# Attention with an expert stage on one core: five token sets for six, and split up-weights kept in DRAM

## The chip, the core and the metric

The kernel runs on one core of a Trainium2 chip. The metric is the time of one execution in device microseconds (us); lower is better. TensorE does the matmuls, VectorE, ScalarE and POOL (GpSimd) the elementwise work, SP (SyncE) issues most DMAs, and POOL issues some on a queue of its own, where descriptors are made in software.

## The reference, cut to what matters

```python
scores = scale * np.matmul(q, k.transpose(0, 1, 3, 2)) + bias.transpose(2, 0, 1)[None]
attn = softmax(scores)                      # batch 8, heads 8, 576 x 576
x = np.matmul(attn, v)                      # gathered to 4608 tokens x 512
a = x @ w1                                  # 512 -> 1024
b = x @ w2                                  # 512 -> 1024
h = a * b @ w3                              # 1024 -> 1024
return h @ w_out                            # 1024 -> 512
```

The weights of the expert stage come as 64-bit floats and are narrowed on the chip.

## The kernel before, in words

Attention runs first, 32 units of one head pair and one batch. It leaves unscaled rows of x (x_d, one tensor for each of four head pairs) and the reciprocal row sums (r_d) in DRAM. Under its end, and after it, w3 and w_out are folded into one down-weight by matmuls (fold, L775; their bank is wacc), so that the expert stage is two products: up (x with w1 and w2, then the product g of both) and down (g with the folded weight).

Every fp32 operand is split into a rounded high part and a low part (split, L904: ScalarE copies, VectorE subtracts), and a product is three matmuls of 128x128 weights with a moving tile of some columns (times, L1053). The expert stage goes over the 4608 tokens in six sets of 768 (TOK, L727). Each set is two halves of 384 tokens, and 384 is the number of columns of a matmul. Up and down are done as 2x2 block products with seven products for eight (seven, L1068; Winograd's form, named "1" to "7"), which needs sums of blocks of both operands. The first set's up-product alone is done with eight (plain_step, L1113), as its weights are just being narrowed: 8 steps of 48 matmuls. Later sets take 8 up steps of 42 matmuls (up_step, L1136) and every set 168 for down (down_step, L1160).

Of a set's x, four rows groups are loaded into the tile xr, and the matching reciprocal sums, broadcast, into xs (fetch in x_units, L922, with load_x, L808, and load_r, L814: one DMA of x and two of r each, all on SP's queue). POOL scales (L819) and makes the block sums (L935), and seven units are split into xu, a ring of nine units. The same ring holds the 14 units of g.

Up-weights: the first set narrows blocks 3 to 7 while it computes (narrowed, L1001: a fetch from the input, two ScalarE, four VectorE and two POOL steps for each half) and stores all eight, unsplit, in wu_d (L1033). Each later set loads each of the eight again, 0.5 MB (L1039), POOL makes four sums (L1045), ScalarE and VectorE split into ub and ut (up_ring, L1037). Down-weights are split once, stored in dw_d and loaded seven times a set, 1 MB each, by POOL's queue (fetch_down, L1224).

Products leave the PSUM banks b through ScalarE's copy into one of eight buffers wos (take, L1063, the copy is L1066); VectorE adds, and SP stores to out from the same buffer (L1187).

A planner (Planner, L112) sets the order on each engine, SP's queue among them. Each step has an engine, a supposed duration, the steps it follows and the ring buffers it takes. A step of a ring takes a buffer when the older one's users are done. The planner walks through time and gives each engine the step that can start first; a DMA is costed on its own, with 0.08 us of its queue and the bytes at a fixed rate, whatever else is in flight:

```python
    def dma(b):
        return 2.3 + b / 300e3
...
            clock[s.on] = t + (0.08 if s.on == "SP" else s.us)
```

TensorE's order is written by hand in the last loop of the kernel (work, L1259 to L1267). Each queue issues in order: an instruction that has to wait holds all that stand behind it.

Of the kernel before, what the change touches and what calls it, by code (L numbers as in the profile page):

```python
# [38 lines left out]
    "r0": 0.0, "r1": 0.9, "r2": 1.8, "r3": 2.7, "h0": 3.6, "h1": 4.5, "h2": 5.4, "h3": 6.3, "l0": 4.5, "l1": 5.4, "l2": 6.3, "l3": 7.2,  # L39
# [5 lines left out]
PRODUCT = {"1": (0, 1), "2": (1, 2), "6": (2, 4), "5": (3, 3), "7": (4, 5), "3": (5, 0), "4": (6, 6)}  # L45
XU_N, SR_N, FIN_N, BANK_N, WU_N, UB_N, UT_N, DW_N = 9, 6, 8, 8, 4, 3, 2, 4
# [55 lines left out]
class Step:  # L102

    def __init__(self, on, us, run, after, uses, takes, lag):
        self.on, self.us, self.run, self.after, self.takes, self.lag = on, us, run, list(after), list(takes), lag
        self.uses = list(uses) + self.takes
        self.then, self.want, self.start = [], None, None
        for h in self.uses:
            h.users.append(self)


class Planner:  # L112

    LAG = {"PE": 0.25, "SP": 0.0}

# [3 lines left out]
    def step(self, on, us, run, after=(), uses=(), takes=(), lag=None):  # L119
        s = Step(on, us, run, [a for a in after if a is not None], uses, takes, self.LAG.get(on, 0.1) if lag is None else lag)  # L120
        self.steps.append(s)
        return s

    def order(self, pe, bank):
# [39 lines left out]
        clock = {}  # L164
# [14 lines left out]
        while len(out) < len(self.steps):  # L179
            best = None  # L180
            for e, cands in ready.items():
                free = clock.get(e, 0.0)
                picks = []
                for s in cands:
                    if e == "PE" and s is not pe[turn]:
                        continue
                    t = max([free] + [done[b] + (b.lag if b.on != e else 0.0) for b in s.after])
# [52 lines left out]
def relpos_attention_moe(  # L240
# [136 lines left out]
    x_d = [dram.tile([P, NTOK], F32, name=f"x_d{p}") for p in range(NPAIR)]  # L377
    r_d = [dram.tile([2, NTOK], F32, name=f"r_d{p}") for p in range(NPAIR)]
# [348 lines left out]
    TOK = 768  # L727
    CH = TOK // 2
    NPR = NTOK // TOK
# [6 lines left out]
    cv = moe.enter_context(tc.tile_pool(name="cv2", bufs=2, side="right"))  # L736
# [3 lines left out]
    wu_d = [dram.tile([P, 2 * DM], F32, name=f"wu_d{t}") for t in range(NF)]  # L740
    dw_d = [dram.tile([P, 2 * KG * BW], F32, name=f"dw_d{i}") for i in range(7)]
# [14 lines left out]
    fo = ExitStack()  # L756
    fp = fo.enter_context(tc.tile_pool(name="fp", bufs=3, side="right"))
# [11 lines left out]

    def ub(i):  # L770
        if "ub" not in late:
            late["ub"] = gp.tile([P, UB_N, 2, 3, BW], F32R, name="ub")
        return late["ub"][:, i]
# [31 lines left out]
    def xa(t, k):  # L805
        return X["x"][:, k * KH:(k + 1) * KH, t * CH:(t + 1) * CH]

    def load_x(c, cc):  # L808
        nc.sync.dma_start(X["x"][:, cc, :], x_d[cc][:, c * TOK:(c + 1) * TOK])

    def flat(i):
        return X["s"][:, i].rearrange("p k n -> p (k n)")

    def load_r(c, cc, i):  # L814
        for h, rows in enumerate((lo, hi)):
            nc.sync.dma_start(flat(i)[rows], r_d[cc][h:h + 1, c * TOK:(c + 1) * TOK].broadcast_to([64, TOK]))  # L816

    def scale(eng, cc, i):
        eng.tensor_tensor(X["x"][:, cc, :], X["x"][:, cc, :], flat(i), op=ALU.mult)  # L819
# [7 lines left out]
    def unit(i, low):  # L827
        return X["u"][:, i, low]
# [17 lines left out]
    X["s"] = xs.tile([P, SR_N, KH, CH], F32, name="xs")  # L846
    X["u"] = xs.tile([P, XU_N, 2, KH, CH], F32R, name="xu")
    ut = xs.tile([P, UT_N, 2, 4, BW], F32R, name="ut")
# [6 lines left out]
    def first_load():  # L855
        for cc in range(NC):
            load_x(0, cc)
            load_r(0, cc, cc)

# [38 lines left out]
    def dma(b):  # L898
        return 2.3 + b / 300e3
# [444 lines left out]
```

## Time and profile before

| | |
|---|---|
| median of 3 runs | 1139.82 us (1139.54 to 1141.91) |
| profiled execution, its own time | 1143.05 us |
| its span | 1141.3 us |
| mean granted TensorE clock | 0.964 |
| busy: TensorE, VectorE, ScalarE, POOL | 92%, 77%, 62%, 52% |
| DMA | 199.79 MB, mean 175 GB/s |

The span goes from the first to the last instruction of the profiled execution; a little time lies around it, so its own time is longer. A busy share is a mean over stages with different limits. Attention and the fold take the span up to about 517 us, the expert stage the rest. An "idle before" with an arrow names what ended the wait.

### The profile page before, as it was taken

How to read it: one execution, taken by the hardware profiler on the slowest of the kernel's cores; microseconds unless marked ns; L12 is line 12 of the kernel's file. 1: busy time of each engine (PE TensorE's matmuls, PEld its weight loads, DVE VectorE, ACT ScalarE, POOL GpSimd, SP SyncE). 2: the span in 40 equal slices, each digit the busy share in tenths (PEclk: the TensorE clock that was granted, in tenths of full speed). 3: DMA queues.
4: the chain of work that ended last, by engine and by line, in shares of the span. 5: the costliest groups of instructions: out<-in, count | busy, mean ns of one | idle time of the engine just before them, and what ended most of it. 6: DMA issues, size and time to landing. Idle time of an engine off the chain costs nothing.

```text
span 1141.3 us, 24384 instructions
## 1 busy us (share of the span) xinstructions
PE 1051.1 (92%) x9448; PEld 913.2 (80%) x9448; DVE 879.8 (77%) x1592; ACT 706.2 (62%) x1292; POOL 588.7 (52%) x486
## 2 busy tenths in 40 slices
PE   6979999999999999997778989979996996999998
PEld 2367777777777777676668979979996996999998
DVE  8958887888888888483898748957885794787775
ACT  8779988998998998552524534624552472455433
POOL 0076766776776775403584357337436542743310
PEclk9989999999999999998888989999998998899999
DMA  7955574566557452158567763592286259228205
GB/s 231 318 162 172 177 238 144 174 211 210 160 174 233 160 172 94 52 155 249 194 239 286 262 191 92 160 288 88 73 277 186 74 177 275 83 61 272 75 1 166
DMA packets 72866, 199.79 MB, mean 175 GB/s; under 512 B 10800, under 2 KB 25520, under 8 KB 66480
## 3 DMA queue, kind: packets, MB, share of 16 engines
q1 hardware_dynamic: 65248, 150.39, 42.3%
q0 software_dynamic: 6496, 45.94, 12.2%
q10 hardware_dynamic: 1008, 1.92, 0.6%
q8 instruction: 74, 1.21, 0.5%
q14 instruction: 40, 0.33, 0.1%
HBM read 156.77 MB, written 41.45 MB: 174 GB/s over the span
## 4 chain that ended last, share of the span: by engine, by line
PE 71%; DVE 12%; DMA 10%; issue 3%; ACT 2%; SPq 2%; POOL 1%; DVEq 0%; ACTq 0%; POOLq 0%
PE b L1055 33%; PE pst L574 14%; PE s L463 13%; PE pst L515 6%; DMA xs<-r_d 5%; PE wacc L798 4%; DVE zdve L665 3%; DMA out_dram<-wos 2%; DVE xu L910 2%; DMA ub<-in_moe_w_dram 1%; DVE ut L910 1%; DMA nb_d<-bev 1%; DVE ub L318 1%; SPq L816 1%; DVE w3s L910 1%
## 5 line engine op out<-in xcount | busy, mean ns | idle before, releaser
L1055 PE MATMUL b<-xu,ut 128*128 128x384 f32 x1344 | 265.5, 349 | 65.6 <-ACT wos L1066 35.6
L1055 PEld LDWEIGHTS b<-xu,ut 128*128 128x128 f32 x1344 | 248.4, 197 | 70.3 <-ACT wos L1066 36.9
L474 DVE CUSTOM_DVE_ANT_0 ts<-s,nb 128x576 f32<-128x576 f32 x288 | 210.6, 756 | 53.7 <-PE s L463 21.3
L499 ACT ACTIVATE pp<-ts,mx 128x576 f32<-128x576 f32 x256 | 195.9, 769 | 17.1 <-DVE mx L474 17.1
L902 DVE TENSOR_TENSOR wos<-b,wos 128x384 f32<-128x384 f32 x156 | 84.4, 553 | 125.1 <-PE b L1055 117.1
L1055 PE MATMUL b<-xu,w3s 128*128 128x384 f32 x1008 | 179.2, 334 | 0.0
L1055 PEld LDWEIGHTS b<-xu,w3s 128*128 128x128 f32 x1008 | 175.4, 188 | 0.0
L574 PE MATMUL pst<-pt,rv 128*64 128x320 f32 (+1 forms) x1280 | 169.3, 411 | 1.3 <-ACT pt L542 1.3
L1066 ACT COPY wos<-b 128x384 f32<-128x384 f32 x183 | 86.6, 477 | 119.4 <-PE b L1055 74.2
L542 ACT ACTIVATE pt<-pst 128x1024 f32<-128x1024 f32 x128 | 128.5, 1021 | 28.4 <-PE pst L515 26.2
L1055 PE MATMUL b<-xu,ub 128*128 128x384 f32 x720 | 141.4, 341 | 0.0
L574 PEld LDWEIGHTS pst<-pt,rv 128*64 128x64 f32 x1280 | 86.3, 136 | 62.4 <-issue 9.7
L1045 POOL TENSOR_TENSOR wi<-wu 128x256 f32<-128x256 f32 x80 | 83.6, 1064 | 99.7 <-DVE ut L910 96.9
L1055 PEld LDWEIGHTS b<-xu,ub 128*128 128x128 f32 x720 | 129.2, 192 | 0.0
L463 PE MATMUL s<-kh,qh 64*128 64x288 f32 x640 | 116.3, 356 | 6.8 <-DVE mx L474 6.7
L822 ACT ACTIVATE ub<-wu 128x768 fp32r<-128x768 f32 x40 | 34.0, 849 | 113.7 <-PE b L1055 101.4
L515 PE MATMUL pst<-ident,pp 64*128 64x64 f32 x2304 | 102.4, 223 | 1.1 <-ACT pt L542 0.6
L515 PEld LDWEIGHTS pst<-ident,pp 64*128 64x128 f32 x2304 | 100.0, 140 | 3.3 <-ACT pt L542 1.2
L540 DVE COPY pt<-pst 64x64 f32<-64x64 f32 (+3 forms) x160 | 82.1, 514 | 25.3 <-PE pst L574 18.9
L463 PE MATMUL s<-kh,ql 64*128 64x288 f32 x640 | 97.2, 294 | 0.9 <-DVE ql L444 0.9
L463 PE MATMUL s<-kl,qh 64*128 64x288 f32 x640 | 97.1, 294 | 0.0
L819 POOL TENSOR_TENSOR xr<-xr,xs 128x768 f32<-128x768 f32 x20 | 39.2, 1961 | 104.4 <-DMA xs<-r_d 104.4
(118 smaller groups left out, 1855.2 us busy)
## 6 DMA issues: line engine op xcount, KB each, us to landing
w3s<-dw_d POOLq DMA_DIRECT2D x42, 1024.0 KB, 6.1
wu<-wu_d SPq DMA_DIRECT2D x40, 512.0 KB
rq<-in_q_dram SPq DMA_DIRECT2D x28, 640.0 KB
wi<-in_moe_w_dram SPq DMA_DIRECT2D x22, 512.0 KB
nb_d<-bev SPq DMA_DIRECT2D x36, 295.5 KB
rv<-in_v_dram SPq DMA_DIRECT2D x32, 320.0 KB
x_d<-pt SPq DMA_DIRECT2D x32, 288.0 KB
xr<-x_d SPq DMA_DIRECT2D x24, 384.0 KB
```

The lines of the kernel that those rows point to most:

```text
L463: nc.tensor.matmul(s[:, hf, :HS], Q[x][rows, q0:q0 + P], K[y][rows, h * HS:(h + 1) * HS], start=(m == 0), stop=(m == len(ops) - 1),)
L474: nc.vector.tensor_tensor_reduce(out=halves(ts), in0=d.pop(("s", t))[:, :, :HS], in1=halves(NB[p, t]), op0=ALU.add, op1=ALU.min, scale=-1. ...
L499: nc.scalar.activation(pp, ts, AF.Exp, bias=mx, scale=-1.0, accum_out=sums[p][:, 9 * b + col:9 * b + col + 1])
L515: nc.tensor.transpose(ps[0:n, hf, c0:c0 + 64], x[rows], ident[rows, rows])
L540: nc.vector.tensor_copy(o, x)
L542: nc.scalar.activation(o, x, AF.Copy)
L574: nc.tensor.matmul(o, x[:, c0:c0 + D], m, start=(c == 0), stop=(c == 4))
L798: nc.tensor.matmul(wacc[ft], l[:, n * P:(n + 1) * P], r[t], start=(t == 0 and m == 0), stop=(t == NF - 1 and m == 2),)
L902: return lambda: nc.vector.tensor_tensor(o(), a(), b(), op=op)
L1045: nc.gpsimd.tensor_tensor(o, x, y, op=ALU.subtract)
L1055: nc.tensor.matmul(acc, w(l), x(r), start=start and i == 0, stop=stop and i == 2, skip_group_check=True)
L1066: return h, pl.step("ACT", 0.16 + CH / 1200, lambda: nc.scalar.copy(fin[h.at], banks[src.at]), after, [src], [h])
```

## The change

Five token sets of 912, 924, 924, 924 and 924 tokens replace six of 768, so a matmul has 456 or 462 columns. The number of matmuls in the expert stage goes from 3072 to 2568 (384 plain, 4 x 336 up, 5 x 168 down).

Split up-weights: the second set loads the unsplit blocks, splits three of them, makes the sums in place and splits these, all in one buffer w of seven blocks (up_sums), and stores that buffer, 1.835 MB, in ws_d. The three sets behind it load whole buffers (up_whole) on POOL's queue and split nothing. The ring w has three buffers; the rings ub and ut go.

From the third set on x and r are loaded by POOL's queue, each of the four behind a load of a weight buffer of the set in front (pace); the second set's are loaded by SP. Scaling and block sums of x move from POOL to VectorE. The ring xu has eight units; four of them, and xr, are lent to the narrowing in the first set, so g is split there only when all blocks are narrowed (first_s). Two of the split down-weights stay in SBUF from the first split on, and their order of making is turned round.

The planner counts transfers: one wire for all DMAs (first byte 2.0 us, then the bytes one after the other), at most eight unfinished DMAs in a queue, and 0.6 us of the queue for each.

```diff
-PRODUCT = {"1": (0, 1), "2": (1, 2), "6": (2, 4), "5": (3, 3), "7": (4, 5), "3": (5, 0), "4": (6, 6)}
-XU_N, SR_N, FIN_N, BANK_N, WU_N, UB_N, UT_N, DW_N = 9, 6, 8, 8, 4, 3, 2, 4
+PRODUCT = {"1": (0, 1), "2": (1, 2), "6": (2, 4), "5": (3, 5), "7": (4, 3), "3": (5, 0), "4": (6, 6)}
+TOKENS = 912, 924, 924, 924, 924
+XU_N, FIRST_U, FIN_N, BANK_N, WU_N, HELD_W, W_N, DW_N = 8, 4, 8, 8, 3, 3, 3, 4
...
+        self.busy = 0.6 * lanes if mb else us
+        self.us = Planner.FIRST_BYTE + mb / Planner.RATE if mb else us
...
+    FIRST_BYTE, RATE, LANES = 2.0, 300e3, 8
...
+                    if s.mb and len(lanes[e]) >= self.LANES:
+                        t = max(t, lanes[e][-self.LANES])
...
-            clock[s.on] = t + (0.08 if s.on == "SP" else s.us)
+            clock[s.on] = t + s.busy
             done[s] = t + s.us
+            if s.mb:
+                wire = max(wire, t + self.FIRST_BYTE) + s.mb / self.RATE
+                done[s] = s.end = wire
+                lanes[s.on] += [wire] * s.lanes
...
     def x_units(c):
...
-            a = pl.step("SP", dma(8 * P * TOK), fetch, takes=[hx, hs] if cc == 0 else [hs], uses=[] if cc == 0 else [hx])
-            r.append(pl.step("POOL", 0.2 + TOK / 467, lambda cc=cc, hs=hs: scale(nc.gpsimd, cc, hs.at), [a], [hx, hs]))
...
+            on, queue = ("SP", nc.sync) if c == 1 else ("POOL", nc.gpsimd)
+            fetch = pl.step(on, 0.0, lambda cc=cc, queue=queue: load_x(queue, c, cc), () if c == 1 else pace[c - 1][cc:cc + 1], [hx] if cc else (), ([] if cc else [hx]) + [hs[cc]], mb=2 * P * TOKENS[c] * 4, lanes=3)
+            r.append(pl.step("DVE", tt(2 * n), lambda cc=cc: scale(nc.vector, c, cc), [fetch], [hx, hs[cc]]))
...
+    def up_sums(n, hw, kept):
+
+        h7 = R["w"].hold()
+        get = pl.step("SP", 0.0, lambda: nc.sync.dma_start(wu[hw.at], wu_d[n]), kept, takes=[hw], mb=512 << 10)
 
         def sums():
...
+            b = blocks(hw.at)
+            for o, x, y in ((2, 0, 2), (0, 1, 0), (1, 1, 2), (3, 3, 1)):
+                nc.gpsimd.tensor_tensor(b[:, o], b[:, x], b[:, y], op=ALU.subtract)
+
+        w = split(lambda: blocks(hw.at)[:, 1:4], 3 * BW, lambda k: w7(h7.at)[:, k, 0:3], h7, [get], [hw], [h7])
+        s = pl.step("POOL", 4.4, sums, w, [hw])
+        w += split(lambda: blocks(hw.at), 4 * BW, lambda k: w7(h7.at)[:, k, 3:7], h7, [s], [hw])
+        put = store(7 << 18, lambda: nc.sync.dma_start(ws_d[n], f(w7(h7.at))), w, [h7])
+        return h7, w, [put]
+
+
+    def up_whole(n, kept):
+        h7 = R["w"].hold()
+        return h7, [pl.step("POOL", 0.6, lambda: nc.gpsimd.dma_start(w7(h7.at), ws_d[n]), kept, takes=[h7], mb=7 << 18)], []
...
+                if c == 0:
+                    after = list(after) + first_s
...
+            if c == 0:
+                rings = [up_sums(n, R["wu"].hold(), kept[n]) for n in range(NF)]
+                kept = [r[2] for r in rings]
+            else:
+                rings = [up_whole(n, kept[n] if c == 1 else ()) for n in range(NF)]
+            pace[c + 1] = [r[1][0] for r in rings]
```

SP's queue before, at the end of a set's down products (out_dram<-wos is the store of a result, wu<-wu_d an up-weight block, xr and xs the loads of x and r for the set after the next up-products):

```order
L1187 DMA out_dram<-wos_9520 128x384
L1039 DMA wu_8970<-wu_d_8977 128x1024
L809 DMA xr<-x_d_85 128x768
L816 DMA xs<-r_d_89 64x768 x2
L809 DMA xr<-x_d_86 128x768
L816 DMA xs<-r_d_90 64x768 x2
L809 DMA xr<-x_d_87 128x768
L816 DMA xs<-r_d_91 64x768 x2
L809 DMA xr<-x_d_88 128x768
L816 DMA xs<-r_d_92 64x768 x2
L1187 DMA out_dram<-wos_9516 128x384
L1187 DMA out_dram<-wos_9517 128x384
```

SP's queue with the change, from the second set's up steps into its down products (ws_d<-w stores a split buffer):

```order
L1066 DMA ws_d_8973<-w_9517 128x3584
L1056 DMA wu_8961<-wu_d_8968 128x1024
L1066 DMA ws_d_8974<-w_9287 128x3584
L1056 DMA wu_83<-wu_d_8969 128x1024
L1066 DMA ws_d_8975<-w_9517 128x3584
L1066 DMA ws_d_8976<-w_9517 128x3584
L1066 DMA ws_d_8977<-w_9287 128x3584
L1212 DMA out_dram<-wos_9523 128x462
L1212 DMA out_dram<-wos_9524 128x462
```

The loads of x and r are gone from this queue, and behind these rows it holds stores of out alone up to its end.

POOL before, from one set's down products to the next set's up steps:

```order
L1231 DMA w3s_9569<-dw_d_8979 128x2048
L1045 TENSOR_TENSOR wi<-wu_9514 128x256 x2
L1045 TENSOR_TENSOR wi<-wu_9514,wi 128x256 x2
L936 TENSOR_TENSOR xr<-xr,xs 128x2x384
L1231 DMA w3s_10058<-dw_d_8980 128x2048
L1231 DMA w3s_10058<-dw_d_8981 128x2048
L1231 DMA w3s_9569<-dw_d_8982 128x2048
L819 TENSOR_TENSOR xr<-xr,xs 128x768 x4
L936 TENSOR_TENSOR xs<-xr 128x768
L1045 TENSOR_TENSOR wi<-wu_83 128x256 x2
```

POOL with the change, the same place of a later set:

```order
L1263 DMA w3s_10106<-dw_d_8982 128x2048
L1263 DMA w3s_10106<-dw_d_8983 128x2048
L1263 DMA w3s_9561<-dw_d_8984 128x2048
L822 DMA xr<-x_d 128x924
L824 DMA xs<-r_d 64x924 x2
L822 DMA xr<-x_d 128x924
L824 DMA xs<-r_d 64x924 x2
L822 DMA xr<-x_d 128x924
L824 DMA xs<-r_d 64x924 x2
L1072 DMA w_9287<-ws_d_8973 128x3584
L1072 DMA w_9517<-ws_d_8974 128x3584
```

POOL's sums and scalings have left it; three of the four loads of x and r now stand here, ahead of the set's fourth weight buffer.

VectorE with the change, among the up steps of the second set (g<-b and wos<-b read banks, w<-wu is a split of weights):

```order
L841 TENSOR_TENSOR w_9517<-wu_8961,w_9517 128x768
L832 TENSOR_TENSOR xr<-xr,xs 128x924
L918 TENSOR_TENSOR wos_9519<-b_9535,wos_9519 128x462
L918 TENSOR_TENSOR wos_9524<-b_9532,wos_9524 128x462
L918 TENSOR_TENSOR wos_9522<-b_9537,wos_9522 128x462
L841 TENSOR_TENSOR w_9517<-wu_8961,w_9517 128x1024
L918 TENSOR_TENSOR g<-b_9535,wos_9519 128x462
L841 TENSOR_TENSOR w_9287<-wu_83,w_9287 128x768
```

The scaling (L832) that POOL did as L819 stands between the two splits of one weight buffer.

## Rows read from the trace of the kernel before

**Rows 1.** The page's head.

```profile
span 1141.3 us, 24384 instructions
```

**Rows 2.** Timeline of TensorE: start, us, instructions merged, idle before and its end.

```profile
516.92 16.81 PE L1055 MATMUL b<-xu,ut 128*128 128x384 f32 x96
546.08 0.69 PE L1055 MATMUL b<-xu,ut 128*128 128x384 f32 x1 [12.35 <-ACT ut L822]
...
623.59 25.12 PE L1055 MATMUL b<-xu,w3s 128*128 128x384 f32 x144
648.55 1.21 PE L1055 MATMUL b<-xu,ub 128*128 128x384 f32 x6
...
771.84 2.29 PE L1055 MATMUL b<-xu,ut 128*128 128x384 f32 x6 [9.07 <-ACT wos L1066]
...
1136.78 0.68 PE L1055 MATMUL b<-xu,w3s 128*128 128x384 f32 x3
```

**Rows 3.** Windows: length, busy PE PEld DVE ACT POOL, clock, DMA share, GB/s.

```profile
495.00:515.00 20.00, 20.00 (x88) 16.30 (x87) 18.25 (x28) 10.71 (x17) 0.00 (x0) 1.00 0.49 121
546.00:623.50 77.50, 60.98 (x288) 58.73 (x289) 72.33 (x72) 31.34 (x49) 52.83 (x36) 0.86 0.66 236
614.00:622.00 8.00, 8.00 (x38) 8.00 (x38) 7.53 (x10) 3.67 (x6) 0.81 (x2) 0.79 1.05 415
623.50:660.00 36.50, 36.50 (x212) 36.50 (x211) 26.68 (x31) 19.27 (x30) 12.36 (x14) 1.00 0.77 257
760.00:780.00 20.00, 10.93 (x54) 10.62 (x54) 6.49 (x8) 4.57 (x8) 14.84 (x11) 0.74 0.66 192
```

**Rows 4.** Waits from 600 us on: us in total, times, longest.

```profile
ACT wos L1066 <- DMA out_dram<-wos: 44.3, 4, 12.9
...
PE b L1055 <- ACT wos L1066: 35.6, 4, 11.4
```

**Rows 5.** Timeline of SP's queue, 745 to 772 us.

```profile
750.26 0.43 SPq L809 DMA_DIRECT2D xr<-x_d  x1
...
761.53 1.94 SPq L816 DMA_DIRECT2D xs<-r_d  x2
764.06 3.60 SPq L1187 DMA_DIRECT2D out_dram<-wos  x4
```

**Rows 6.** The chain of waits, 500 to 800 us, the fold's end.

```profile
499.97 16.42 PE wacc L798 x71
```

**Rows 7.** Lines by shape (busy, mean ns); VectorE, POOL, ScalarE; last: POOL's timeline.

```profile
L318 DVE TENSOR_SCALAR wmag<-wmag 128x512 f32<-128x512 f32 x1 | 0.4, 420 | 0.0
...
L825 DVE TENSOR_TENSOR xu<-xr,xu 128x768 fp32r<-128x768 f32 x4 | 3.6, 954 | 0.0
...
L318 DVE TENSOR_SCALAR ub<-ub 128x512 f32<-128x512 f32 x7 | 9.7, 1391 | 0.0
...
L902 DVE TENSOR_TENSOR g<-b,wos 128x384 f32<-128x384 f32 x13 | 7.1, 549 | 3.3 <-ACT wos L1066 3.3
...
L910 DVE TENSOR_TENSOR ut<-wi,ut 128x1024 fp32r<-128x1024 f32 x4 | 4.9, 1216 | 0.0
...
L345 POOL TENSOR_TENSOR wu<-wu,ub 128x512 f32<-128x512 f32 x8 | 14.1, 1764 | 15.7 <-DVE ub L340 10.8 <-issue 2.6 <-ACT wos L1066 2.3
...
L819 POOL TENSOR_TENSOR xr<-xr,xs 128x768 f32<-128x768 f32 x2 | 3.6, 1824 | 52.9 <-DMA xs<-r_d 52.9
L345 POOL TENSOR_TENSOR wu<-wu,ub 128x512 f32<-128x512 f32 x2 | 2.5, 1262 | 0.0
...
L822 ACT ACTIVATE ut<-wi 128x1024 fp32r<-128x1024 f32 x2 | 2.1, 1064 | 0.3 <-PE b L1055 0.3
...
774.52 1.43 POOL L1045 TENSOR_TENSOR wi<-wu 128x256 f32<-128x256 f32 x2
```

**Rows 8.** The line of POOL's loads of dw, whole span: ns min/median/max; us to landing.

```profile
L1231 POOL DMA_DIRECT2D w3s<-dw_d x42: 530/530/601, 608.6 to 1121.1; - x42
...
DMA to landing us min/median/max: 5.1/6.1/12.9
```

More of the change, by code (lines that the diff above doesn't have):

```diff
@@ L114, with step @@
     LAG = {"PE": 0.25, "SP": 0.0}
+    FIRST_BYTE, RATE, LANES = 2.0, 300e3, 8
     def __init__(self):
         self.steps = []
-    def step(self, on, us, run, after=(), uses=(), takes=(), lag=None):
-        s = Step(on, us, run, [a for a in after if a is not None], uses, takes, self.LAG.get(on, 0.1) if lag is None else lag)
+    def step(self, on, us, run, after=(), uses=(), takes=(), lag=None, mb=0, lanes=1):
+        s = Step(on, us, run, [a for a in after if a is not None], uses, takes, self.LAG.get(on, 0.1) if lag is None else lag, mb, lanes)
         self.steps.append(s)
@@ L724, in relpos_attention_moe @@
     att_r.close()
-    TOK = 768
+    NPR = len(TOKENS)
+    assert sum(TOKENS) == NTOK
+    AT = [sum(TOKENS[:c]) for c in range(NPR)]
+    TOK = max(TOKENS)
     CH = TOK // 2
-    NPR = NTOK // TOK
+    HALF = [n // 2 for n in TOKENS]
     KH = NC // 2
@@ L1011, in part, with go @@
                 fns[i]()
-            def go(on, us, i, after, takes=(), part=part, hc=hc, hw=hw):
-                return pl.step(on, us, lambda: part(i), after, [h for h in (hc, hw) if h not in takes], takes)
-            fetch = go("SP", dma(512 << 10), 0, (), [hc] + ([hw] if m == 0 else []))
+            def go(on, us, i, after, takes=(), part=part, hc=hc, **more):
+                return pl.step(on, us, lambda: part(i), after, [h for h in (hc, hw) if h not in takes], takes, **more)
+            fetch = go("SP", 0.0, 0, (), [hc] + ([hw] if m == 0 and not more else []), mb=512 << 10)
@@ L1055, in times, with bank, spare, take @@
             nc.tensor.matmul(acc, w(l), x(r), start=start and i == 0, stop=stop and i == 2, skip_group_check=True)
[L1057 to L1063 removed]
+    def bank(h, n):
+        return lambda: banks[h.at][:, 0:n]
+    def spare(h, n):
+        return lambda: fin[h.at][:, 0:n]
+    def take(src, after, n):
         h = R["fin"].hold()
[L1066 to L1068 removed]
+        return h, pl.step("ACT", 0.16 + n / 1200, lambda: nc.scalar.copy(spare(h, n)(), bank(src, n)()), after, [src], [h])
+    def seven(n, make, ends, parts=1):
         acc, d, s = {}, {}, {}
@@ L1182, in ends @@
                     e = d[what] = R["fin"].hold()
-                    done = pl.step("DVE", tt(CH), lambda: nc.vector.tensor_copy(fin[e.at], banks[h.at]), [done], [h], [e])
+                    done = pl.step("DVE", tt(nh), lambda: nc.vector.tensor_copy(spare(e, nh)(), bank(h, nh)()), [done], [h], [e])
                 else:
-                    d[what], done = take(h, [done])
+                    d[what], done = take(h, [done], nh)
             e = d[what]
-            pl.step("SP", dma(4 * P * CH), lambda: nc.sync.dma_start(rows, fin[e.at]), [done], [e])
@@ L1189, in down_step @@
-        return seven(make, ends, 2)
+            store(4 * P * nh, lambda: nc.sync.dma_start(rows, spare(e, nh)()), [done], [e])
+        return seven(nh, make, ends, 2)
     def split_down():
         blk = {(a, b): wf[:, a, b].rearrange("p k n -> p (k n)") for a in range(2) for b in range(2)}
-        got, prev = {}, {}
-        def sub(o, x, y, after):
-            return pl.step("DVE", tt(KG * BW), on_v(lambda: blk[o], lambda: blk[x], lambda: blk[y], ALU.subtract), after)
+        got = {}
@@ L1207, in operand @@
             i = "1256734".index(which)
-            got[which] = (h, l, pl.step("SP", dma(1 << 20), lambda: nc.sync.dma_start(dw_d[i], f(dw(hs.at)).rearrange("p l n -> p (l n)")), [h, l], [hs]))
+            kept = store(1 << 20, lambda: nc.sync.dma_start(dw_d[i], f(dw(hs.at)).rearrange("p l n -> p (l n)")), [h, l] + gates[len(got):len(got) + 1], [hs] + held_as)
+            got[which] = (h, l, kept, *held_as)
             return [h, l]
-        one = operand("1", (0, 0), ())
-        two = operand("2", (1, 0), ())
+        stay = {which: R["dw"].hold(at=i) for i, which in enumerate("12")}
```

299 lines of the change are left out of this document (151 added, 148 removed).

## The prediction

> **What bounds the kernel now.** I read the page first: the span is 1141.3 us [rows 1], and TensorE is the engine that the end hangs on. So I went to the timeline of TensorE and cut the expert stage in two. The fold ends and the first token set begins at 516.92; the first down product begins at 623.59; the last matmul ends at 1137.46, and 3.8 us of stores follow [rows 2]. 3072 matmuls of 384 columns lie in there. What one costs without a wait is read where 144 stand without a gap, 623.59 to 648.55: 173.3 ns, at a granted clock of 1.00 [rows 2, 3]. The first set is 384 matmuls, or 66.5 us of work, and takes 106.7: 40.2 us are lost. The other 2688 are 465.8 us of work and take 513.9: 48.1 us are lost. The question is only what becomes of these 88.3 us.
>
> The two losses differ. In the first set the wait before 546.08 is 12.35 us [rows 2]; from there to its end VectorE is busy for 72.33 of 77.5 us and POOL for 52.83 [rows 3], so each block of up-weights comes late. In the later sets the view of waits shows four waits, 35.6 us in all, for a copy of ScalarE into wos, and that copy waited 44.3 us in four waits for the store to out [rows 4]. The queue of SP says why: from 750.26 on it issues the twelve loads of x and r for a later set, each held back in turn, and only at 764.06 the four stores of out that stand behind them [rows 5]. TensorE sits still for 9.07 us, until 771.84 [rows 2], and in the slice with that wait the mean granted clock is 0.74 instead of 1.00 [rows 3]: matmuls at the lower level (of 1.2 and 2.4 GHz) stand behind each wait and are the rest of the 48.1.
>
> **The change, part by part.** *Five sets for six.* 2568 matmuls replace 3072, but they are wider: 384 + 168 of 456 columns and 2016 of 462 (1344 up, 672 down). One could hope that 504 fewer instructions save their start. The rows say no: 71 matmuls of 512 columns took 16.42 us [rows 6], 231.3 ns each, so 0.452 ns a column, and 384 columns cost 0.451. Time goes with columns. At 0.4515 ns, 456 are 205.9 ns and 462 are 208.6. The first set becomes 79.1 us, its down products 34.6, each later set 504 x 0.2086 = 105.1, four of them 420.5. In all 534.2 against 532.4: the change costs TensorE 1.8 us, because more tokens go the plain way.
>
> *Fold.* The four first loads grow by 912/768, and eight VectorE steps of 954 ns [rows 7] grow by 0.18 each, 1.4 us, while VectorE is busy for 18.25 of 20 us [rows 3]. Between 0 (hidden) and 3.7 us (1.4, and 2.3 for 0.59 MB more at the 257 GB/s of 623.5 to 660 [rows 3]) I take 1.
>
> *SP's queue.* From the third set on SP holds nothing but stores of out; x, r and the weights go out on POOL's queue. No store stands behind a load then, so the four waits and their slow matmuls, 48.1 us, go. The x of the second set is loaded on SP during the first set, well ahead of stores.
>
> *First set and its down products.* The fetches of raw weights now lie ahead of the loads of x, and four fit at once, so the wait before 546.08 goes. What then decides is VectorE with POOL. VectorE's steps that read two SBUF operands, or run at the double rate, grow when POOL computes: 420 ns became 1391, and POOL's 1262 became 1764 [rows 7]; a VectorE step that reads a bank stayed at 549. From 546 to 623.5 I priced the instructions at what they take alone (VectorE: 23 TENSOR_SCALAR at 0.42, 16 steps of 1024 elements at 1.22, 11 of 768 at 0.954, 8 of 512 at two thirds of that, 13 from banks at 0.549: 51.9 us; POOL: 16 of 512 at 1.262, 11 sums of 256 at half of 1.43, five of 768 at 1.824: 37.2) [rows 7]. Their sum is 89.1 and the stage took 77.5, so the two together get by with 0.87 of their sum. In the order of the changed kernel I count for VectorE, from the first plain product to the end of the down products, 30 TENSOR_SCALAR, 21 steps of 1024, 37 of 912 or 924, three of 768, 10 of 512 and 22 from banks, 104 us by the same prices, since the scaling and sums of x come to it; for POOL 20 of 512 and 12 of 256, 33.8. That makes 137.8 x 0.87 = 119.9 us against 113.7 of TensorE: 6 us late. The bounds are 0 (hidden, as part of it is needed by the next set only) and 24.1 (all in turn).
>
> *The second set's up-weights.* A buffer of w is filled in a chain in place: copy, subtraction, four sums on POOL, copy, subtraction. Alone that is 0.8 + 0.95 + 4 x 0.715 + 1.06 + 1.22 = 6.9 us [rows 7]. TensorE holds a buffer for 12 groups of six, 15.0 us, out of a cycle of three steps of 42, 26.3 us; 11.3 are left. So 0 is one bound; if each of five hand-overs waits behind one step of 1.22 us that stands in front, the chain is 13.0, 1.7 late in each of five refills, and 8.5 is the other. I take 4, between them.
>
> *The three sets behind it.* Eight loads of 1.835 MB replace eight of 0.52 MB and all splitting. Per set 8 x 1.835 + 7 x 1.05 + 3.8 + 1.9 = 27.8 MB in 105.1 us, 264 GB/s; with loads of dw in flight the engines moved 415 GB/s [rows 3]. Such a load has the same 11.3 us. A load of dw, 1 MB, lands in 6.1 us (5.1 to 12.9), and its issue takes POOL 530 ns [rows 8]: times 1.75 that is 10.7, with the issue 11.2. It just fits. The scaling by bytes alone is cautious, as the 5.1 us hold a part that does not grow. I take 2 us for three sets; the bounds are 0 and, at 22.6 us a load, 15 x 11.8 = 177. The ScalarE and VectorE splits that go away are worth nothing of their own: both had spare time there.
>
> **Sum.** 516.9 + 1 + 79.1 + 34.6 + 420.5 + 3.8 = 1055.9; with 6, 4 and 2 us of waits 1067.9 of span. The profiled execution took 1143.05, 1.75 above its span, and lies 3.2 above the median of 1139.82. So 1066 for a median.
>
> **Rivals.**
> *POOL and VectorE in turn.* If nothing overlaps, the first set and its down products take the full 137.8: 24 instead of 6, and 1084. For it: 420 ns that became 1391. Against it: the 0.87, and bank readers at 549 ns beside POOL [rows 7]. The Trainium skill, "SBUF — State Buffer", section "SBUF: two separate sides", calls the port pair that the two share an exclusive lock; by that rule the 24 would stand, and this trace, with 77.5 us for 89.1 of work, agrees only in part.
> *Software queue held up.* POOL must issue the whole weight stream while VectorE, which now has x's scaling too, is busy. If each issue waits for a VectorE step in front (up to 2 us, one of 1024 elements beside 0.8 of a wait of its own), a load comes at 13.2, 1.9 late, fifteen times: 29 us, 1095. Against it: 42 issues beside a busy VectorE took 530 to 601 ns, none more [rows 8]. The same page and section warns that DMAs from GpSimd's queue wait for descriptors while VectorE holds the shared ports, and advises the other queues; it speaks against this change, and the 601 ns speak against the rule here.
> *The stores were not the cause.* If the copies into wos wait as before for another reason, 48.1 stay: 1114. Against it: four of four waits name the store [rows 4].
> *Slower than before.* The stream of w is late as a whole: POOL's queue is one line, and a load of w stands behind nine loads of x and r or behind dw. Fifteen loads decide. They eat the 73 us gained when each comes 4.9 later than the 11.3, at 16.2 us; the 12.9 of one dw load, times 1.75, is past that, and would give 1066 + 175 = 1241. Against it: the median of 6.1, and SP's loads, which now don't compete.
>
> **How the numbers follow.** My forecast, 1053 to 1080, gets 0.67; in turn 0.13; held up 0.07; stores not the cause 0.06; slower 0.05; 0.02 for no change. A measurement of this kernel can tell 0.2%, 2.3 us, from nothing; all cases but the last two are far below. So faster 0.93, same 0.02, slower 0.05. The likeliest case gives 1066. Downwards only the 1 us of the fold and the 12 of waits can be missing: 1053. Upwards the range takes in the first two rivals and a mix of them, 1105; the other cases, 0.13, stay out.
>
> **What would show it.** Right: matmuls of 462 columns at 208 to 209 ns and about 105 us from set to set; no wait of TensorE for ScalarE behind a store; SP's queue without long waits; the first set at 80 to 88 us; VectorE close to 95% until the up-products of the second set. Wrong: TensorE waiting for w behind a load, in steps of 8.8 us (the stream is late), issues on POOL well over 0.6 us (held up), or first down products later than 105 us after the fold (in turn). A clock under 1.00 in the later sets would mean that waits have come back.

## The result, and the profile after

The changed kernel takes **1069.84 us** (median of 4 runs, 1068.83 to 1073.83) against 1140.87 for the kernel before in the same session (4 runs): a ratio of 0.938, interval 0.935 to 0.941. The forecast was 1066 with a range of 1053 to 1105. The profiled execution took 1068.83 us.

The page of the changed kernel begins so (busy time, share of the span, instructions):

```profile
span 1067.1 us, 22794 instructions
...
PE 1038.4 (97%) x8944; PEld 847.5 (79%) x8944; DVE 807.7 (76%) x1485; ACT 640.4 (60%) x1175; POOL 418.7 (39%) x369
```

The span is 74.2 us shorter than that of [rows 1]. The timeline of TensorE from the fold's end says where; its columns are those of [rows 2]:

```profile
517.21 79.54 PE L1077 MATMUL b<-xu,w 128*128 128x456 f32 x384
598.14 0.47 PE L1077 MATMUL b<-xu,w3s 128*128 128x456 f32 x1 [1.39 <-ACT w3s L838]
599.40 16.54 PE L1077 MATMUL b<-xu,w3s 128*128 128x456 f32 x71 [0.79 <-DVE w3s L841]
616.15 5.20 PE L1077 MATMUL b<-xu,w3s 128*128 128x456 f32 x24 [0.21 <-DMA w3s<-dw_d]
622.90 10.17 PE L1077 MATMUL b<-xu,w3s 128*128 128x456 f32 x48 [1.54 <-ACT wos L1088]
...
640.39 43.14 PE L1077 MATMUL b<-xu,w 128*128 128x462 f32 x204
684.05 21.77 PE L1077 MATMUL b<-xu,w 128*128 128x462 f32 x102 [0.51 <-DVE wos L918]
...
853.55 64.49 PE L1077 MATMUL b<-xu,w 128*128 128x462 f32 x306
...
959.50 64.39 PE L1077 MATMUL b<-xu,w 128*128 128x462 f32 x306
...
1030.04 33.02 PE L1077 MATMUL b<-xu,w3s 128*128 128x462 f32 x156
```

All 384 products of the first set stand in one row without a gap: the 12.35 us of [rows 2], and the smaller waits behind it, are gone. Four short waits are left in its down products, one of 0.51 us in the second set, and from 684 us on there is none. From 853.55 to 959.50, the same place of two sets, are 105.95 us.

Windows of the last stretch that waits, columns as in [rows 3]:

```profile
560.00:580.00 20.00, 20.00 (x99) 18.19 (x98) 19.15 (x21) 6.85 (x9) 9.31 (x5) 1.00 0.96 278
580.00:600.00 20.00, 17.82 (x86) 15.66 (x85) 19.37 (x20) 9.13 (x12) 6.48 (x5) 1.00 0.74 279
600.00:620.00 20.00, 19.79 (x89) 17.51 (x88) 19.89 (x20) 12.15 (x16) 8.37 (x9) 0.91 1.02 374
620.00:640.00 20.00, 18.46 (x90) 16.43 (x89) 17.92 (x20) 10.76 (x15) 7.63 (x7) 1.00 0.75 285
```

VectorE (third pair) is busy for 95% of the first set's end and its down products. Of these four windows the granted clock is under 1.00 only in 600 to 620, behind the waits; 0.91 is a mean over matmuls at the upper and the lower of the two levels (2.4 and 1.2 GHz). The stream of split blocks is seen in the page's costliest groups and its DMA issues (issue time and mean ns; KB, median us to landing):

```profile
L1072 POOL DMA_DIRECT2D w<-ws_d x24 | 13.0, 541 | 197.3 <-PE b L1077 197.3
...
w<-ws_d POOLq DMA_DIRECT2D x24, 1792.0 KB, 8.2
w3s<-dw_d POOLq DMA_DIRECT2D x33, 1024.0 KB, 9.2
```

An issue took 541 ns in the mean, and a load landed in 8.2 us (median). The 24 issues lie between 695 and 1004 us; from 747 to 1005 VectorE was busy for 155.7 of 258 us.

### The profile page after: what moved, and what is told of

It is laid out like the page before. It is cut to its first block, busy times and chain, and to the rows that moved or that the text cites. A ratio compares the mean times of both kernels' runs of the same rounds, so it can differ in the third digit from the quotient of the medians.

```text
span 1067.1 us, 22794 instructions
## 1 busy us (share of the span) xinstructions
PE 1038.4 (97%) x8944; PEld 847.5 (79%) x8944; DVE 807.7 (76%) x1485; ACT 640.4 (60%) x1175; POOL 418.7 (39%) x369
## 4 chain that ended last, share of the span: by engine, by line
PE 86%; DVE 7%; DMA 3%; ACT 1%; issue 1%; POOL 1%; SPq 0%; ACTq 0%; DVEq 0%; POOLq 0%
PE b L1077 45%; PE pst L587 15%; PE s L476 13%; PE pst L528 6%; PE wacc L810 4%; DVE zdve L678 4%; DMA w3s<-dw_d 1%; POOL wu L1061 1%; DMA nb_d<-bev 1%; PE pst L535 1%; PE pst L541 1%; DVE ts L487 0%; ACT pt L555 0%; DVE g L918 0%; DVE w3s L841 0%
## 5 line engine op out<-in xcount | busy, mean ns | idle before, releaser
L1077 PE MATMUL b<-xu,w 128*128 128x462 f32 (+1 forms) x1728 | 365.9, 372 | 0.5 <-DVE wos L918 0.5
L1077 PEld LDWEIGHTS b<-xu,w 128*128 128x128 f32 x1728 | 325.1, 188 | 37.9 <-DVE wos L918 0.9
L1077 PE MATMUL b<-xu,w3s 128*128 128x462 f32 (+1 forms) x840 | 181.9, 374 | 3.9 <-ACT wos L1088 1.5
L1088 ACT COPY wos<-b 128x462 f32<-128x462 f32 (+1 forms) x151 | 81.0, 542 | 171.3 <-PE b L1077 170.1
L1077 PEld LDWEIGHTS b<-xu,w3s 128*128 128x128 f32 x840 | 159.1, 190 | 23.6 <-ACT wos L1088 1.9
L918 DVE TENSOR_TENSOR wos<-b,wos 128x462 f32<-128x462 f32 (+1 forms) x126 | 79.7, 637 | 122.1 <-PE b L1077 116.9
L838 ACT ACTIVATE xu<-g 128x924 fp32r<-128x924 f32 (+1 forms) x60 | 55.7, 968 | 78.5 <-DVE g L918 78.5
L460 POOL TENSOR_TENSOR ql<-rq,qh 128x1280 fp32r<-128x1280 f32 x31 | 91.2, 2944 | 2.6
L476 PEld LDWEIGHTS s<-kh,qh 64*128 64x128 f32 x640 | 64.7, 193 | 25.9 <-DVE pt L553 10.8
L841 DVE TENSOR_TENSOR xu<-g,xu 128x924 fp32r<-128x924 f32 (+1 forms) x60 | 66.6, 1148 | 5.9 <-ACT xu L838 5.9
```

The costliest lines, as they stand in the source:

```text
L460: nc.gpsimd.tensor_tensor(l, x, f(h), op=ALU.subtract)
L476: nc.tensor.matmul(s[:, hf, :HS], Q[x][rows, q0:q0 + P], K[y][rows, h * HS:(h + 1) * HS], start=(m == 0), stop=(m == len(ops) - 1),)
L841: nc.vector.tensor_tensor(o, x, f(h), op=ALU.subtract)
L918: return lambda: nc.vector.tensor_tensor(o(), a(), b(), op=op)
L1077: nc.tensor.matmul(acc, w(l), x(r), start=start and i == 0, stop=stop and i == 2, skip_group_check=True)
L1088: return h, pl.step("ACT", 0.16 + n / 1200, lambda: nc.scalar.copy(spare(h, n)(), bank(src, n)()), after, [src], [h])
```

## The experiments

Twelve kernels ran, each beside the kernel before (medians 1142.3 to 1143.8). A line of dots in a piece of code stands for lines left out. The fold's end, where the code hardly differs, lay between 516.5 and 521.7 us in these profiles, so for small differences I also give the **expert stage**: from the first up-product to the span's end. In the changed kernel it is 1067.1 - 517.2 = 549.9 us.

### Is the width worth anything? Six sets in the changed kernel

```
-TOKENS = 912, 924, 924, 924, 924
+TOKENS = 768, 768, 768, 768, 768, 768
```

> The changed kernel with six sets of 768 tokens for its five; queues, kept blocks and counting stay. In TensorE's work six sets are the cheaper: 384 matmuls of 173.3 ns, 168 of 173.3 and 2520 of 173.3 are 532.4 us, where the changed kernel's own rows come to 538 (its 462 columns took 210.4 ns). Theory A (the queues made the gain, the sets are only wider cover): the first set has 95.6 us of TensorE to hide about 112 of VectorE with POOL (x's share of their work shrinks, the weights' share does not), so 16 us late where the changed kernel is 7; a buffer of w is free for 21.8 - 12.5 = 9.3 us where a load lands in 8.2 and is issued in 0.5, so loads just fit or come some tenths late, 0 to 10 us in all. 1064 + 9 + 0 to 10: 1070 to 1085. Theory B (the wider sets are the gain, as fewer matmuls or fewer fetches of weights): most of the 71 us come back, 1110 or more. Theory C (width is worth nothing at all): 1064, faster than the changed kernel by its dearer columns.

Measured: 1079.97 us, ratio 0.9446 (0.9418 to 0.9475); stage 563.6. Theory A. Two of the waits on TensorE's timeline:

```profile
618.24 9.45 PE L1077 MATMUL b<-xu,w3s 128*128 128x384 f32 x42 [6.83 <-ACT wos L1088]
...
1036.92 7.56 PE L1077 MATMUL b<-xu,w 128*128 128x384 f32 x42 [0.60 <-DMA w<-ws_d]
```

From 516.97 to 633.82 stand 564 matmuls of 173.3 ns, 97.7 us, so the first set with its down products is 19.1 us late where five sets are 7. The loads of w do come late, but by tenths. The stage is 13.7 us longer although its matmuls are 5 us less: 12 us lie in the first set, and in the later sets about 8 us are lost, of which waits make 3.0 (1.7 for loads of w, 1.3 for VectorE's sums). Five sets are worth 10 us, though they cost TensorE more: mostly as cover for VectorE and POOL in the first set.

### Was it SP's queue? Only the loads of x moved, in the kernel before

```
-                load_x(c, cc)
-                load_r(c, cc, hs.at)
+                load_x(c, cc, nc.gpsimd)
+                load_r(c, cc, hs.at, nc.gpsimd)
...
```

The step that issues them is planned on POOL.

> The kernel before, with one thing altered: the loads of x and r of all later sets are issued on POOL's queue and no longer on SP's, so no store of out stands behind them. Theory A (stores behind loads made the four waits): the 35.6 us of waits for ScalarE's copies into wos and the slow matmuls behind them, 48.1 together, go; 1141 - 36 to 48 is 1093 to 1105. Theory B (the copies wait for another reason, for instance because the stores themselves are late): 1141, with the waits for wos where they were. Theory C (POOL's order takes SP's place: its sums of up-weights stand behind a load that waits for its buffer): the waits for wos go, and waits for w or ut of the same size come, 1125 to 1141 or more.

Measured: 1118.5 us, ratio 0.9799 (0.9763 to 0.9835). None of the three. Waits behind the first set, of TensorE and of the copies into wos, and the window in which the kernel before stood:

```profile
PE b L1055 <- DVE wos L902: 11.3, 7, 3.0
PE b L1055 <- ACT wos L1066: 8.1, 8, 2.1
ACT wos L1066 <- DMA out_dram<-wos: 28.3, 12, 3.6
```

```profile
760.00:780.00 20.00, 19.03 (x108) 18.39 (x106) 19.24 (x19) 8.89 (x14) 19.81 (x12) 1.00 0.17 53
```

The four waits of [rows 4] shrink from 35.6 us to 8.1 in pieces of at most 2.1, so the stores behind loads were what made them long; copies still wait 28.3 us for stores, but in twelve pieces. And 11.3 us of waits for VectorE's sums take their place, with VectorE busy for 19.24 and POOL for 19.81 of 20 us in this window, and much the same in 860 to 880 and 960 to 980. Behind the first set 616.42 to 1112.37 is 496.0 us for 465.8 of work: 30 us are still lost of 48. The queue alone is worth 18 us there, and 7 in the first set (99.3 us for 106.7). The 48 were not one loss.

### Undone in the changed kernel: queue, counting, both

```
-on, queue = ("SP", nc.sync) if c == 1 else ("POOL", nc.gpsimd)
+on, queue = "SP", nc.sync
```

> The changed kernel with the loads of x and r of the third to fifth set back on SP's queue, among the stores of out; all else stays, the counting of transfers too. Theory A (the queue alone decides): each of three sets has its twelve loads in front of stores again, as the four waits of the kernel before, 9 to 12 us each, come back for three: 1070 + 27 to 36 is 1097 to 1106. Theory B (it is the counting, by which the planner sees that a load holds up the stores behind it and puts it elsewhere): 1070, with no wait of TensorE for a copy into wos.

Measured: 1069.92 us, ratio 0.9365 (0.9347 to 0.9382); stage 548.9. Theory A falls: with the loads of x back among the stores, TensorE does not wait from 640 us on.

```
-self.busy = 0.6 * lanes if mb else us
-self.us = Planner.FIRST_BYTE + mb / Planner.RATE if mb else us
+self.busy = (0.08 if on == "SP" else 0.6) * lanes if mb else us
+self.us = 2.3 + mb / Planner.RATE if mb else us
...
-if s.mb and len(lanes[e]) >= self.LANES:
-    t = max(t, lanes[e][-self.LANES])
...
```

> The changed kernel, with the planner's account of transfers as it was before: each takes 2.3 us and its bytes at the same rate whatever else is in flight, and there is no limit to how many one queue holds. Only the order of instructions can differ. Theory A (the queues and buffers decide, and a load goes out when its buffer is free whatever the plan thinks): 1070, within 3 us. Theory B (the counting decides): loads stand in an order that blocks others; then TensorE waits behind a store or a load of w in steps of some us for each later set, 1085 to 1120.

Measured: 1078.41 us, ratio 0.9442 (0.9419 to 0.9465); stage 559.4. Neither theory: 8.6 us are more than A allows, and they lie in another place than B said, ahead of 680 us. The longest waits on TensorE's timeline:

```profile
610.61 1.06 PE L1073 MATMUL b<-xu,w3s 128*128 128x456 f32 x2 [3.10 <-ACT xu L834]
...
629.49 10.24 PE L1073 MATMUL b<-xu,w3s 128*128 128x456 f32 x48 [2.59 <-ACT wos L1084]
...
656.82 17.94 PE L1073 MATMUL b<-xu,w 128*128 128x462 f32 x84 [2.03 <-DVE wos L914]
```

All its waits sum to 11.7 us, 7.2 more than the changed kernel's. The counting earns its gain in the first and second set, where raw weights, x and down-weights are all on the way, and nothing later.

> Both undone in the changed kernel: the loads of x and r of the later sets are on SP's queue among the stores of out, and the planner's account of transfers is the old one. With the loads on SP but counted the time was 1070, as with neither undone; uncounted but with the loads on POOL it was 1078, and the 8.5 us more lay ahead of 680 us, in the first set, its down products and the second set; from there on TensorE never waited. Theory A (for the later sets queue and counting are two cures of one thing, either suffices): with neither, stores stand behind held loads again, the waits for copies into wos come back for three sets, 9 to 12 us each: 1078 + 27 to 36 is 1105 to 1114. Theory B (what cured the later sets is neither, but the buffers: x's scale rows have four of their own now, and no load waits for one that the steps of the set still use): 1078, with no such wait behind 680.

(Both edits together.) Measured: 1082.77 us, ratio 0.9468 (0.9448 to 0.9489); stage 562.8. Nearer to theory B: 4.4 us over the run before, but no wait of TensorE behind 690 us. So a third thing kept the later sets whole. A window at the loads of x gave a hint: in 750 to 770 us the DMA engines of the kernel before were busy 1.07 of the time, here 0.94:

```profile
756.00:776.00 20.00, 20.00 (x96) 17.84 (x96) 9.05 (x11) 5.88 (x11) 0.53 (x1) 1.00 0.94 283
```

In the kernel before seven loads of dw go out between 725 and 753 us, straight before and among the loads of x; in the changed kernel each waits for a load of w to be through, by a line of the change that neither its description nor the prediction mentions.

### The loads of dw unpaced

```
-                last + [g[2] for g in got.values()][:5] if got else pace[c][min(5 + i, 7):][:1], takes=[hw], mb=1 << 20,
+                last + [g[2] for g in got.values()][:5] if got else [], takes=[hw], mb=1 << 20,
```

First on top of the two edits before, then alone.

> The changed kernel with three things undone together: the loads of x and r of the later sets on SP's queue among the stores of out, the old account of transfers, and now also no pacing of the loads of dw, which so far each waited for a load of w to be through. With the first two undone the time was 1083 and TensorE never waited behind 690 us. In the kernel before, four loads of dw fell on the same stretch as the loads of x (735 to 770), the DMA engines were busy 1.05 to 1.10 of the time there, and SP's queue stood; with the pacing two fell there, at 0.53 to 0.87. Theory A (the crowd of dw loads beside those of x made the stores late; pacing is the second cure): waits for copies into wos of some us come back at each of three sets: 1083 + 15 to 36 is 1098 to 1119. Theory B (three sets later the loads of dw have nothing to collide with, as the raw up-weights no longer come by SP): 1083, no wait. Theory C (unpaced loads of dw stand ahead of the loads of w on POOL's queue): TensorE waits for w, in steps of 1 to 6 us, not for copies.

Measured: 1101.84 us, ratio 0.9645 (0.9621 to 0.9669); stage 583.6, so 20.8 us more than with the first two undone. Theory A, with the waits in another place: they end at VectorE. The views are the window, the waits behind 640 us, VectorE's timeline and the longest wait on TensorE's:

```profile
760.00:780.00 20.00, 19.37 (x93) 16.98 (x92) 4.38 (x6) 5.35 (x9) 1.06 (x2) 1.00 1.05 309
```

```profile
PE b L1073 <- DVE wos L914: 16.8, 6, 10.3
...
DVE xr L828 <- DMA xs<-r_d: 48.0, 9, 17.3
```

```profile
772.87 1.12 DVE L828 TENSOR_TENSOR xr<-xr,xs 128x924 f32<-128x924 f32 x1 [7.71 <-DMA xs<-r_d]
...
779.80 1.12 DVE L828 TENSOR_TENSOR xr<-xr,xs 128x924 f32<-128x924 f32 x1 [5.26 <-DMA xs<-r_d]
```

```profile
664.81 19.61 PE L1073 MATMUL b<-xu,w 128*128 128x462 f32 x84 [10.29 <-DVE wos L914]
```

Seven loads of dw go out from 733.9 to 766.7 us, the engines are full (1.05), r lands late, and since the scaling of x is now VectorE's, the sums into wos stand behind it in VectorE's queue. SP's twelve loads of x and r take from 760.0 to 780.2 us, where they took from 756.3 to 767.3 with the pacing. The longest wait, 10.3 us, lies in the second set, where the run before had one of 3.9 at the same place; the others lie in the third and fourth set (774.60 to 888.09, the same place of the two, are 113.5 us for 105.95). Theory B of the run before, that x's scale rows have four buffers of their own now, can't be the whole: they were there here too. What they add was not run.

> The changed kernel with the pacing of the loads of dw alone undone: the loads of x and r stay on POOL's queue, transfers stay counted. With all three undone the time was 1102, 19 us over the run with the first two undone; the lost time stood at 654 (10.3 us) and around 775 to 790 and 888 to 902, where VectorE stood at the scaling of x until r had landed, up to 17.3 us. Theory A (the pacing is what keeps the later sets whole, since a late load of x holds VectorE's queue whichever queue carries it): 10 to 20 us come back, 1080 to 1090, with VectorE waiting for xs. Theory B (queue and counting are a cure of their own): 1070, no wait behind 690. Theory C (on POOL's queue the bunched loads of dw now stand ahead of those of x and w): TensorE waits for w as well, above 1090.

Measured: 1074.54 us (1071.28 to 1080.05), ratio 0.9398 (0.935 to 0.9447); stage 553.8, 4 more than the changed kernel, in a run whose times lie 9 us apart. Nearer to B, with a little of C; the two waits behind 640 us:

```profile
PE b L1077 <- DMA w<-ws_d: 1.6, 1, 1.6
PE b L1077 <- DVE wos L918: 1.5, 1, 1.5
```

So for the later sets there are two cures, the pacing on the one hand and the queue with the counting on the other, each nearly enough alone. Stage times in us:

```
                                   dw paced    dw unpaced
x on POOL's queue, counted           549.9        553.8
x on SP's queue, counted             548.9      (not run)
x on POOL's queue, uncounted         559.4      (not run)
x on SP's queue, uncounted           562.8        583.6
```

### Are the kept split blocks worth anything?

```
-            if c == 0:
-                rings = [up_sums(n, R["wu"].hold(), kept[n]) for n in range(NF)]
-                kept = [r[2] for r in rings]
-            else:
-                rings = [up_whole(n, kept[n] if c == 1 else ()) for n in range(NF)]
+            rings = [up_sums(n, R["wu"].hold(), kept[n] if c == 0 else ()) for n in range(NF)]
...
-        put = store(7 << 18, lambda: nc.sync.dma_start(ws_d[n], f(w7(h7.at))), w, [h7])
...
```

> The changed kernel without the kept split blocks: every later set fetches the raw up-weights (0.52 MB in place of 1.835), splits them, forms their sums on POOL and splits those, as the second set does; the eight stores of split blocks go too. All else stays. Theory A (the refill chain fits, as the second set shows with 0.5 us of waits; the kept blocks save nothing on the path): 1070, within 4. Theory B (the chain fits only where VectorE and POOL have nothing else to do; in the later sets it shares them with the scaling and the sums of x and the splits of g): TensorE waits for w in steps of 1 to 3 us, 5 to 8 us a set as the kernel before still had with its loads moved off SP: 1085 to 1094.

Measured: 1071.67 us (1070.2 to 1072.67), ratio 0.9369 (0.935 to 0.9388); stage 551.1; no wait behind 640 us. Theory A. The page counts 186 MB moved for the changed kernel's 232. The part of the change named second in its title, blocks kept in DRAM, shows as 1.2 us between the stages and 1.8 between the medians, which these runs can't tell from nothing.

### What is late in the first down products?

```
-GATE = 5
+GATE = 10
```

> The changed kernel, with the stores of the split down-weights no longer held back until the fetches of the last raw up-weights are through. In the changed kernel the first set's down products wait four times, 1.4, 0.8, 0.2 and 1.5 us, and a load of dw between them takes 15.8 us from issue to landing. Theory A (the loads of dw come late because their stores went late): the third wait and part of the fourth go, 1 to 2 us: 1068. Theory B (VectorE with POOL is what is late there, the transfers have time): 1070, unchanged. Theory C (the stores take the raw weights' share of the DMA engines and the first set's later blocks come late): waits of 1 to 3 us in the first set, 1072 or more.

Measured: 1069.91 us (1067.86 to 1071.19), ratio 0.9353 (0.9333 to 0.9373); stage 550.2. Theory B has the number, but its reason is not tested: counted from the first up-product, the six stores of dw go out at 43 to 83 us here and at 43 to 82 in the changed kernel. The hold that was taken away had not held them, and what earlier stores would do stays open.

```
+            if c == 1:
+                r.append(pl.step("POOL", 0.2 + 2 * n / 467, lambda cc=cc: scale(nc.gpsimd, c, cc), [fetch], [hx, hs[cc]]))
+            else:
...
```

The four sums of the second set's x are moved in the same way.

> The changed kernel, with the eight steps that scale and sum the second set's x (1.1 us each on VectorE without neighbours, 1.1 to 2.2 in place) moved from VectorE to POOL, where by the rows of 768 elements at 1.82 us one of 924 takes 2.19. They lie between 572 and 630 us, where the first set's down products wait 4 to 7 us in all. Theory A (VectorE is the bound there and POOL has room): VectorE gets 9 us back, the waits of the first down products shrink to 0 to 2: 1063 to 1066. Theory B (the two share one budget, 0.87 of their sum): 8.5 us more of work in all, 7 us later: 1077. Theory C (the waits are ScalarE's order and the loads of dw, neither of the two): 1070.

Measured: 1076.7 us (1073.48 to 1077.68), ratio 0.9422 (0.9398 to 0.9445). Theory B, with its number. POOL's group of such steps from 560 to 650 us, the sums of the windows from 560 to 660 us, of this kernel and then of the changed one:

```profile
L832 POOL TENSOR_TENSOR xr<-xr,xs 128x924 f32<-128x924 f32 x4 | 11.7, 2942 | 8.0 <-DVE g L918 8.0
```

```profile
sum 100.00, PE 90.36 PEld 80.95 DVE 86.33 ACT 42.80 POOL 55.98; mean PE 18.07 PEld 16.19 DVE 17.27 ACT 8.56 POOL 11.20
```

```profile
sum 100.00, PE 96.08 PEld 85.68 DVE 86.33 ACT 45.89 POOL 40.33; mean PE 19.21 PEld 17.14 DVE 17.27 ACT 9.18 POOL 8.07
```

POOL took 2942 ns for a step estimated at 2.19 us, and VectorE, rid of eight steps, was busy for the same 86.33 us of the 100. Over the whole span its page counts 809.7 us in 1477 instructions, for 807.7 in 1485: its other steps grew by what it had given away. Nothing was gained by moving the work. The Trainium skill, "SBUF — State Buffer", section "SBUF: two separate sides", says that an instruction of either that takes the port pair which the two share locks the other out for its whole length; this run agrees with it in direction. That the busy times add up to 142 us of 100 means overlap or an instruction counted while it is blocked; no run here separates these.

### What does a column cost?

```
-TOKENS = 912, 924, 924, 924, 924
+TOKENS = 896, 928, 928, 928, 928
```

A second kernel has 928, 920, 920, 920, 920.

> The changed kernel with sets of 896, 928, 928, 928 and 928 tokens for 912 and four of 924: matmuls have 448 and 464 columns for 456 and 462. Nothing else changes. Theory A (a column costs 0.4515 ns as at 384 and 512, but widths that are not a multiple of 16 pay a little more: 456 took 206.7 ns, 0.453 a column, and 462 took 210.4, 0.455): 448 columns take 202.3 and 464 take 209.5; 552 x 202.3 + 2016 x 209.5 is 534.0 us where the changed kernel's rows give 538.3, so 4 us less, and 1 us back as the first set is 2 us shorter and its VectorE work hardly: 1066 to 1067. Theory B (it is not the width but what runs beside it, or the price rises between 456 and 512 with the bank's fill): 0.455 a column stays, 464 take 211.3 and the time is 1070 or 1071.

> The changed kernel with sets of 928 and four of 920: matmuls of 464 and 460 columns for 456 and 462. The run with 448 and 464 gave 202.5 and 210.0 ns a matmul, and the changed kernel's 462 took 210.3, so 462 costs what 464 does. The first set becomes wider: its 552 matmuls take 210.0, 2.1 us more of cover for the same work of VectorE on weights, so its waits shrink by up to 2. Theory A (the price goes in steps, 460 still pays for 464): 2016 x 210.0 is 423.4 for 424.0, and the time 1069 to 1070. Theory B (the price is smooth, 0.4515 ns a column and a fixed surplus of at most 1 ns for odd widths): 460 takes 207.7 to 208.7, 3 to 5 us less, and the time 1064 to 1067.

Measured: 1067.24 us (1064.63 to 1068.69), ratio 0.9329 (0.9308 to 0.935), stage 547.5, for 448 and 464 columns; 1066.74 us (1064.45 to 1067.26), ratio 0.9331 (0.9309 to 0.9353), stage 547.2, for 464 and 460. The same row of the last set in each:

```profile
956.80 64.42 PE L1077 MATMUL b<-xu,w 128*128 128x464 f32 x306
```

```profile
958.24 64.09 PE L1077 MATMUL b<-xu,w 128*128 128x460 f32 x306
```

In the changed kernel 306 of 462 took 64.39. From set to set, divided by 504, it is 105.84 and 210.0 ns for 464 columns, 105.95 and 210.2 for 462, 105.14 and 208.6 for 460. So 462 columns cost what 464 do. In the first run theory A has the number but not the reason, since 464 columns are no cheaper than 462: of the 2.4 us by which its stage is shorter, 1.0 lie in the first set with its down products and 1.1 in the second set, which does not wait here. In the second it is theory B: 460 is cheaper by 1.6 ns a matmul. Both versions are 2.4 to 2.7 us shorter in the stage than the changed kernel; their intervals and its own (0.935 to 0.941) just touch, so that they beat it is likely and not settled. No version with a clear lead was found.

## Why the prediction was right, and where it was not

The time came out 3.8 us over the forecast, and the span, 1067.1, 0.8 under the forecast's 1067.9. The two differ because the forecast put the median 1.5 us below the span, as for the kernel before (1066.4, rounded), while here the profiled run was the fastest of four and the median lies 2.7 above the span. The span is closer than its terms were, and in part by luck.

*Fold.* 1 us was taken; the first product began at 517.21 for 516.92, 0.3.

*First set and its down products.* Right in size, and the reason given stood up to two runs. From 517.21 to 640.39 are 123.2 us for 116.2 of work (with the second set's first twelve): 7 us late where 6 were forecast from 0.87 of VectorE's and POOL's work; 3.9 of them are the four waits, and about 2 the matmuls at a granted clock of 0.91 behind them. The rule held nearly when it was loaded from either side: less cover (six sets) gave 19 where it said 16, and work moved onto POOL gave 6.9 more where it said 7. The waits sit wholly in the down products, and the up-products run without a gap. Of the 33 us gained in this stage, 12 went with the wider set and some with the counting. No run undid the lent buffers or the early fetches of raw weights, so that these took away the wait before 546.08 is argued and not shown.

*SP's queue.* The step that failed. It said that 48.1 us go since no store stands behind a load of x any more. They went, but not by this alone: in the kernel before the queue alone gave back 18 of the 48, and in the changed kernel it can be undone at no loss. That the stores behind loads made the four waits long is shown. What the prediction missed is what slowed the loads, seven loads of dw that filled the DMA engines just ahead of them, and that the change paces these: in the changed kernel that is shown (20.8 us come back with it undone on top of queue and counting), in the kernel before the pacing was not tried. It also took VectorE's new work on x as a burden alone. In the kernel before POOL did it, and with the queue cured POOL was full at the place where TensorE still waited; putting it back for one set cost 6.9 us. That this is the rest of the 48 in every set is argued from there, not shown.

*Second set's up-weights.* 4 us were taken between 0 and 8.5; 0.5 was measured, and that was a wait for a sum of VectorE, none for w. The chain fits, and it fits in every set (the run without kept blocks).

*The three sets behind it.* 2 us were taken, 0 came. The load was estimated at 10.7 us by scaling a landing of 6.1 with its bytes; 8.2 was measured (13.4 at most), so 2.5 us of the 11.3 are left in hand at the median. The rival of a stream that comes late as a whole had no ground.

*Columns.* The term that was mis-sized the other way: 462 columns at 208.6 ns, measured 210.2, 3.2 us over 2016 matmuls. From 640.39 to the last matmul's end at 1063.06 are 422.7 us, where matmuls at 208.6 and the 6 us of waits would be 424.0. So the waits that did not come and the dearer columns nearly cancelled. That 504 fewer matmuls save nothing was right: six sets are 5 us less of matmuls, and five are faster all the same.

*Rivals.* "In turn" fell with 7 us for 24, though the two engines do hold each other up in part; its 24 also counted 22 steps that read banks, which the prediction had at an unchanged 549 ns beside POOL. "Software queue held up" fell with issues of 541 ns and no wait of TensorE for w; of the warning of the Trainium skill that the prediction named with it ("SBUF — State Buffer", "SBUF: two separate sides") the issues show nothing, and whether part of the 8.2 us to landing is such a wait the trace doesn't tell. "The stores were not the cause" fell for the four waits, and had a point for the 30 us that stayed when they were cured.

*Signs.* Of those named, VectorE at 95%, issues under 0.6 us, a clock of 1.00 in the later sets, no copy into wos that waits for a store, and about 105 us from set to set (105.95) came. The first set took 79.5 us, just under the 80 to 88, and the matmuls of 462 columns missed their 208 to 209 ns.

## What to carry to other kernels

When a queue stands still, ask what made its transfers slow before moving them to another queue: here spreading a burst of loads cured the later sets as well as the other queue did together with the counting. Count an engine's cover before its work: fewer, wider sets cost TensorE time and won 10 us, since the work on weights that runs beside them does not grow with the width. And where two engines hold each other up, as VectorE and POOL did, price them by one sum, and measure before you expect a gain from moving work between them.

## What the runs showed of the hardware that was not expected

A matmul of 462 columns took as long as one of 464 (210.2 and 210.0 ns), while 460 took 208.6; 384 had taken 173.3. A load of 1.835 MB landed in 8.2 us in the median where one of 1.05 MB took 9.2 in the same profile, so the bytes alone don't set the time; that what else was in flight does is likely, but not separated here.
